# One core, linear attention into two mixtures of experts: where three engines scale the last rows, and eight dummy matmuls for fourteen

## The chip, the cores and the metric

The kernel runs on one core of a Trainium2 chip. A core has five engines, each with its own queue of instructions: TensorE (PE: matmuls and transposes; the profile lists its weight loads apart, as PEld), VectorE (DVE), ScalarE (ACT), GpSimd (POOL) and SyncE (SP, which here issues loads). They wait for one another by semaphores. The metric is the device time of one execution in microseconds (us); lower is better. TensorE's clock has two levels, and the profile gives the granted clock as a share of the full one: 1.00 is 2.4 GHz, 0.50 is 1.2 GHz.

## The reference

```
kv  = einsum('bhsd,bhse->bhde', k, v)         # 4 batches, 8 heads, 576 rows, 64 columns
out = q @ kv                                  # per batch and head
x   = out / sqrt(mean(out^2) + 1e-6) * g_norm # rows of 512 = 8 heads x 64
# mixture of experts, 8 experts, one per token (argmax of x @ w_gate), capacity limited
h = relu(x_e @ w1[e]);  y = h @ w2[e];  x = gate * y
# last layer: maximum of three products, then the output product
out = max(x @ m2w1, x @ m2w2, x @ m2w3) @ w_out    # 2304 x 512
```

## The kernel before, in words

The program has three parts. The first, up to about 91 us, is the attention: four batches one after another, each of 576 rows in five sets (set 0 has 64 rows, sets 1 to 4 have 128). The second, up to about 310 us, runs the experts, the fullest guess first; the third is the last layer. Only the first part and its seam to the second are touched.

For one batch `b` the engines do this. `kv_step` multiplies k and v on TensorE (`pk`, line 348). `out_step` transposes q in five pieces (`pq`, lines 375 and 380), which are copied out of PSUM as `qT`, some by ScalarE (line 386) and some by VectorE (line 384). `out_pair` and `out_rest` make the output products `po` (lines 436 and 408); ScalarE squares them (`sq`) and copies them (`ohl`). VectorE sums the squares (`ss`) and runs `stats_steps`: the norm factor `rnorm` (line 482), the logits (`lt`, `lg`), and the choice of expert (`eq` twice, `rm`, `oh`, lines 494 to 501). `normalise` then scales the five sets into `orow`: on GpSimd or VectorE one instruction for a set (line 516), on ScalarE eight (line 514, one for a head).

The routing of a batch stands inside the next batch's `out_pair`: TensorE makes `pp` (line 531) from `oh`, VectorE turns it into positions (`pt`, `jr`, `oht`, `ohsum`, `pos_i`), TensorE makes the census product `pc` (line 605) from `ohsum`, and VectorE goes on with `ch_v` and `pb`. `send` then hands five scatters of `orow` to memory (`xs`, line 538) to GpSimd's queue; each also waits for a ScalarE copy, so that they spread out.

The rows of the first expert don't go through memory for the later batches. For batches 0 and 1, `own_gather` gathers them back from `xs` into `oxg` (line 598, on GpSimd's queue); its indices are four small VectorE instructions, `og_u` to `og_i` (lines 592 to 595), and it waits for all scatters so far. For batches 2 and 3, `own` makes a 0/1 table on VectorE (`jl`, line 578, then `pick`, line 582), and TensorE picks the rows with it: 20 matmuls `px` (line 660), which the trace counts as 40 passes. For batches 0 and 1 TensorE transposes `oxg` (line 655). `own_out` copies each `px` as the high half (ScalarE, line 666) and the low half (VectorE, line 667) of `xt`, the input of the first expert.

Weights come from memory as raw tiles, four at a time in flight; `split_next` splits one half of a tile into a high part on ScalarE (line 297) and a low part on VectorE (line 298), and when both halves are done the next load is issued. Behind the last `xt`, VectorE makes `po_i` (line 1020), three register loads on ScalarE's queue read it, and then ScalarE copies the first product `ph` of the experts out as `h`.

Dummy matmuls of 128x128 (`keep_warm`, line 331, two passes each) stand at several places in the attention part.

The order on each engine is the order in which the code issues the instructions (the schedule is manual), so moving a call moves its instructions on every engine that it uses.

Of the kernel before, what the change touches and what calls it, by code (L numbers as in the profile page):

```python
# [9 lines left out]
F32 = mybir.dt.float32  # L10
# [11 lines left out]
B, H, S, D = 4, 8, 576, 64  # L22
# [18 lines left out]
def kernel(  # L41
# [16 lines left out]
    nc = tc.nc  # L58
# [40 lines left out]
    ps_o = stA.enter_context(tc.tile_pool(name="ps_o", bufs=6, space=PSUM))  # L99
# [228 lines left out]
    def keep_warm(p_, n):  # L328

        for _ in range(n):  # L330
            nc.tensor.matmul(p_[:, 0:128], ident, ident, start=True, stop=True)

    def kv_step(b):

        pk = ps_kv.tile([128, 4, D], F32, tag="pk", name=f"pk{b}")
        kt = [ins_t["k", b, u] for u in range(3)]
        vt = [ins_t["v", b, u] for u in range(3)]

        order = [(s, 4 * u + h) for u in range(2) for s in (1, 2, 3, 4) for h in range(4)]
        order += [(0, h) for h in range(H)]  # L340
        for s, h in order:
            if b == 0 and h % 4 == 0 and s == 1:
                keep_warm(ps_o.tile([128, 512], F32, tag="po", name=f"warm{h}"), 4 if h else 9)
            if b == B - 1 and h == 4 and s == 1:
                keep_warm(ps_o.tile([128, 512], F32, tag="po", name="warm3"), 8)
            l, r_ = (t_[h // 4][:, h % 4, s - 1, :] if s else t_[2][:, h, :] for t_ in (vt, kt))
            o_ = pk[h % 2 * D:h % 2 * D + D, h // 2, :]
            nc.tensor.matmul(o_, l, r_, start=s == 1 and h < 2, stop=s == 0 and h > 5)
        t_ = sa.tile([128, 4, D], F32, tag="kvT", bufs=1, name=f"kvT{b}")
        drip(b, nc.scalar.activation(out=t_, in_=pk, func=AF.Copy))  # L350
        kvT[b] = t_
# [14 lines left out]
    def out_step(b):  # L366
        qT = {}

        def tr(u):

            pq = ps_o.tile([128, 4, 128], F32, tag="po", name=f"pq{b}{u}")
            if u < 4:
                qm = ins_t["q", b, u % 2]
                for h in range(4):
                    nc.tensor.transpose(pq[:, h, :], qm[:, h, u // 2 * 2:u // 2 * 2 + 2, :], ident)
                n = 128
            else:
                n = D
                for j in range(4):
                    nc.tensor.transpose(pq[:, j, 0:D], ins_t["q", b, 2][:, 2 * j:2 * j + 2, :].rearrange(  # L380
                        "p h d -> p (h d)"), ident[:D, :D])
            t_ = sa.tile([128, 4, 128], F32, tag="qT", bufs=5, name=f"qT{b}{u}")[:, :, 0:n]
            if u == 2 or u == 4 and b < B - 1:
                nc.vector.tensor_copy(t_, pq[:, :, 0:n])
            else:
                i_ = nc.scalar.activation(out=t_, in_=pq[:, :, 0:n], func=AF.Copy)
                drip(b, i_)
            qT[u] = t_

        if b in (0, B - 1):  # L390
            keep_warm(ps_o.tile([128, 512], F32, tag="po", name=f"warmq{b}"), 10 if b == 0 else 6)
        tr(0)
        tr(2)
        if b == 0:
            keep_warm(ps_o.tile([128, 512], F32, tag="po", name="warmr"), 8)
        kvx_step(b)
        tr(1)
        tr(3)
        tr(4)
        return qT  # L400
# [103 lines left out]
    def rows_of(s):  # L504
        return 128 if s else D

    def normalise(b, s, eng):

        n = rows_of(s)
        i_ = ohl[b % 2][:n, s, :, 0:D]  # L510
        o_, r_ = orow[b % 2][:n, s].rearrange("p (h d) -> p h d", d=D), rnorm[b][:n, s]
        if eng is nc.scalar:
            for h in range(H):
                nc.scalar.activation(out=o_[:, h], in_=i_[:, h], func=AF.Copy, scale=r_[:, h:h + 1])
        else:
            eng.tensor_tensor(out=o_, in0=i_, in1=r_.unsqueeze(2).to_broadcast([n, H, D]), op=ALU.mult)
# [36 lines left out]
    def drip(b, i_):  # L553

        if pending:
            scatter(*pending.pop(0))
            after(xs_scatters[-1], [i_], "spread out")
# [29 lines left out]
    def own_gather():  # L587

        V = nc.vector
        u_, m_ = (sl_.tile([128, 2], F32, name=x) for x in ("og_u", "og_m"))  # L590
        i_ = sl_.tile([128, 2], I32, name="og_i")
        V.tensor_scalar(out=u_, in0=pb[:, 0:2], scalar1=slot[:, 0:1], scalar2=None, op0=ALU.add)
        V.tensor_tensor(out=m_, in0=u_, in1=pb[:, 1:3], op=ALU.is_lt)
        V.scalar_tensor_tensor(out=m_, in0=u_, scalar=eb0, in1=m_, op0=ALU.add, op1=ALU.mult)
        V.tensor_scalar_add(i_, m_, float(ZROW))
        for b in range(2):
            oxg[b] = sa.tile([128, DM], F32, tag="oxg", bufs=2, name=f"oxg{b}")
            g_ = nc.gpsimd.indirect_dma_start(
                out=oxg[b][:RB[b]].bitcast(I32), out_offset=None, in_=xs,
                in_offset=IndirectOffsetOnAxis(ap=i_[:RB[b], b:b + 1], axis=0))  # L600
            after(g_, xs_scatters, "rows come from every scatter")
# [62 lines left out]
    def own_out(b, px):  # L664
        at = slice(RO[b], RO[b] + RB[b])
        nc.scalar.activation(out=x0[:, :, 0, at], in_=px, func=AF.Copy, scale=g2)  # L666
        nc.vector.scalar_tensor_tensor(out=x0[:, :, 1, at], in0=px, scalar=g2, in1=x0[:, :, 0, at].bitcast(F32),
                                       op0=ALU.mult, op1=ALU.subtract)
# [12 lines left out]
    SORD = (0, 4, 1, 2, 3)  # L681
# [4 lines left out]
    def routes(b):  # L686
        route(b)
        send(b)

    def census_of(b):  # L690
        pcs[b] = census_pe(b)

    for b in range(B - 1):
        qT = out_step(b)
        out_pair(b, 0, qT, (lambda: routes(b - 1), lambda: census_of(b - 1)) if b else ())
        out_pair(b, 1, qT)
        out_rest(b, qT)
        load_batch(b + 2)
        if b:
            census(b - 1, pcs[b - 1])  # L700
        if b == 1:
            raw_upto(4)
        if b == 2:
            own_gather()
        for _ in stats_steps(b, 0, 5, rnorm[b]):
            pass
        for s in range(5):
            normalise(b, s, nc.gpsimd)
        kv_step(b + 1)
    b = B - 1  # L710
    qT = out_step(b)
# [15 lines left out]
    next(steps)  # L727
    for _ in steps:
        pass
    for s, eng in zip(SORD, (nc.scalar, nc.scalar, nc.gpsimd, nc.gpsimd)):  # L730
        normalise(b, s, eng)
    keep_warm(ps_o.tile([128, 512], F32, tag="po", name="warm6"), 4)
    pc = ps_kv.tile([128, NE], F32, tag="pm", name="pc")
    route(b)
# [3 lines left out]
    keep_warm(ps_o.tile([128, 512], F32, tag="po", name="warm7"), 3)  # L738
    own(b)
    send(b)  # L740
    normalise(b, SORD[4], nc.vector)
    for b_ in (2, 0, 1):
        own_out(b_, pxs[b_])
    split_next(4)
    own_out(b, own_pe(b))
    while pending:
        scatter(*pending.pop(0))
    stA.close()
# [327 lines left out]
    for j in range(NYB):  # L1076
# [20 lines left out]
        for g in range(NG):  # L1097
            jt = j * NG + g
            po = ps_tile(f"pz{jt}")
# [190 lines left out]
```

## Time and profile before

| | us |
|---|---|
| median of three runs | 658.71 (654.8 to 662.6) |
| the profiled execution | 655.94 |
| its span | 654.2 |

| engine | busy, us | share of the span |
|---|---|---|
| PE | 624.2 | 95% |
| DVE | 346.0 | 53% |
| ACT | 270.8 | 41% |
| POOL | 202.5 | 31% |

Times in all rows are counted from the start of the span. A row of the timeline has its start, how long it lasted from its first to its last instruction, the engine, the line, and behind `xN` in brackets how long the engine had been idle and what ended that. A row of the chain has the start and the length of one piece of the chain of work that ended last. A PE row's end is modelled.

### The profile page before, as it was taken

The numbers are of one execution on the slowest core, as the hardware profiler recorded it, in microseconds if no ns is written. First come the engines' busy times: TensorE is split into PE (matmuls) and PEld (weight loads), VectorE is DVE, ScalarE is ACT, GpSimd is POOL, SyncE is SP. The second block draws the span as 40 slices with busy tenths as digits, with TensorE's granted clock in tenths as the row PEclk, the third lists the DMA queues.
The fourth block names the chain that finished last, engine by engine and source line by source line (L and its number), as shares of the span: only waits on it lengthen the run. The fifth ranks groups of instructions, "written<-read, shape, count | busy, mean of one in ns | idle before, by whom it ended". The sixth has DMA issues, their size and how long they took to land.

```text
span 654.2 us, 11325 instructions
## 1 busy us (share of the span) xinstructions
PE 624.2 (95%) x4125; PEld 596.1 (91%) x4125; DVE 346.0 (53%) x719; ACT 270.8 (41%) x619; POOL 202.5 (31%) x280
## 2 busy tenths in 40 slices
PE   8889799989999999999999999999999999999992
PEld 8778798989999999998999989989989989999992
DVE  2576858786989898999965322222222221221220
ACT  1766544765756666676653221121121121121110
POOL 3274853213767685959500010010010001001001
PEclk9999789998999999999999999999999999999997
DMA  8999247866888887888862000000000000000000
GB/s 224 274 327 312 101 138 231 244 220 211 249 255 262 248 271 235 282 254 283 208 188 65 1 33 16 1 26 24 1 17 33 0 17 33 0 18 33 1 17 35
DMA packets 81661, 88.11 MB, mean 135 GB/s; under 512 B 15357, under 2 KB 71165, under 8 KB 81602
## 3 DMA queue, kind: packets, MB, share of 16 engines
q1 hardware_dynamic: 68448, 66.64, 34.8%
q0 software_dynamic: 6240, 14.41, 6.3%
q10 hardware_dynamic: 6914, 6.30, 2.8%
q8 instruction: 34, 0.56, 0.4%
q14 instruction: 25, 0.20, 0.1%
HBM read 71.56 MB, written 15.76 MB: 133 GB/s over the span
## 4 chain that ended last, share of the span: by engine, by line
PE 76%; DVE 9%; DMA 7%; issue 2%; ACT 2%; SPq 2%; ACTq 0%; POOL 0%; DVEq 0%; POOLq 0%
PE pa L762 11%; PE pa L764 11%; PE pa L763 11%; PE py L763 5%; PE py L764 5%; PE py L762 4%; PE pz L1104 4%; PE pz L1103 4%; PE pz L1105 4%; DMA raw<-in_moe_w_dram 3%; DVE w L298 3%; PE ph L764 3%; PE ph L763 3%; PE ph L762 3%; PE px L660 2%
## 5 line engine op out<-in xcount | busy, mean ns | idle before, releaser
L763 PE MATMUL pa<-ys,w 128*128 128x384 f32 x432 | 144.3, 334 | 0.0
L762 PE MATMUL pa<-ys,w 128*128 128x384 f32 x432 | 144.3, 334 | 0.0
L764 PE MATMUL pa<-ys,w 128*128 128x384 f32 x432 | 144.3, 334 | 0.0
L298 DVE TENSOR_TENSOR w<-raw,w 128x512 fp32r<-128x512 f32 x152 | 114.1, 779 | 26.8 <-ACT w L297 26.2
L1108 POOL DMA_INDIRECT out_dram<-o,ctab x18 | 17.5, 972 | 300.2 <-ACT o L1107 297.0
L1091 DVE TENSOR_TENSOR m<-pa,m 128x384 f32<-128x384 f32 x36 | 20.1, 558 | 138.3 <-PE pa L764 138.3
L297 ACT ACTIVATE w<-raw 128x512 fp32r<-128x512 f32 x152 | 89.4, 623 | 8.2 <-DMA raw<-in_moe_w_dram 8.2
L763 PE MATMUL py<-h,w 128*128 128x324 f32 (+7 forms) x256 | 80.9, 316 | 6.5 <-DVE h L786 6.5
L1093 ACT ACTIVATE g<-m 128x384 fp32r<-128x384 f32 x36 | 18.9, 526 | 151.3 <-DVE m L1092 151.3
L763 PEld LDWEIGHTS pa<-ys,w 128*128 128x128 f32 x432 | 81.1, 188 | 0.2
L762 PEld LDWEIGHTS pa<-ys,w 128*128 128x128 f32 x432 | 81.1, 188 | 0.2
L764 PEld LDWEIGHTS pa<-ys,w 128*128 128x128 f32 x432 | 81.1, 188 | 0.0
L763 PE MATMUL ph<-xt,w 128*128 128x324 f32 (+7 forms) x256 | 79.6, 311 | 0.8 <-DVE xt L678 0.6
L762 PE MATMUL py<-h,w 128*128 128x324 f32 (+7 forms) x256 | 80.3, 314 | 0.0
L762 PE MATMUL ph<-xt,w 128*128 128x324 f32 (+7 forms) x256 | 79.4, 310 | 0.6 <-ACT xt L666 0.6
L764 PE MATMUL py<-h,w 128*128 128x324 f32 (+7 forms) x256 | 79.9, 312 | 0.0
L764 PE MATMUL ph<-xt,w 128*128 128x324 f32 (+7 forms) x256 | 79.4, 310 | 0.0
L763 PEld LDWEIGHTS py<-h,w 128*128 128x128 f32 x256 | 48.8, 191 | 9.3 <-DVE h L786 9.1
L915 POOL TENSOR_TENSOR d<-d 128x256 f32<-128x256 f32 x48 | 31.7, 660 | 67.0 <-issue 18.6
L763 PEld LDWEIGHTS ph<-xt,w 128*128 128x128 f32 x256 | 48.3, 189 | 1.4 <-DVE xt L678 0.9
L762 PEld LDWEIGHTS ph<-xt,w 128*128 128x128 f32 x256 | 48.3, 189 | 0.9 <-ACT xt L666 0.8
L762 PEld LDWEIGHTS py<-h,w 128*128 128x128 f32 x256 | 48.7, 190 | 0.2
(247 smaller groups left out, 1052.7 us busy)
## 6 DMA issues: line engine op xcount, KB each, us to landing
raw<-in_moe_w_dram SPq DMA_DIRECT2D x64, 512.0 KB, 4.4
d<-in_moe_w_dram SPq DMA_DIRECT2D x36, 256.0 KB, 5.7
m2w<-dw ACTq DMA_DIRECT2D x36, 128.0 KB, 4.3
raw<-m2w SPq DMA_DIRECT2D x9, 512.0 KB, 4.6
k<-in_k_dram SPq DMA_DIRECT2D x8, 512.0 KB, 7.9
v<-in_v_dram SPq DMA_DIRECT2D x8, 512.0 KB, 9.6
q<-in_q_dram SPq DMA_DIRECT2D x8, 512.0 KB, 8.5
d<-in_moe_w_out_dram SPq DMA_DIRECT2D x12, 256.0 KB, 5.3
```

Source lines behind the costliest of these rows:

```text
L297: nc.scalar.activation(out=hi, in_=src, func=AF.Copy)
L298: (eng or nc.vector).tensor_tensor(out=lo, in0=src, in1=hi.bitcast(F32), op=ALU.subtract)
L762: nc.tensor.matmul(po, lhi, rhi, start=first, stop=False)
L763: nc.tensor.matmul(po, lhi, rlo, start=False, stop=False)
L764: nc.tensor.matmul(po, llo, rhi, start=False, stop=last)
L915: nc.gpsimd.tensor_tensor(out=lo.bitcast(F32), in0=hi.bitcast(F32), in1=lo.bitcast(F32), op=ALU.mult)
L1091: nc.vector.tensor_tensor(out=m_, in0=pa[1][:, :YB], in1=m_, op=ALU.max)
L1093: nc.scalar.activation(out=t_[:, 0], in_=m_, func=AF.Copy)
L1103: nc.tensor.matmul(po, h_[:, 0], w_[:, 0], start=c == 0, stop=False)
L1104: nc.tensor.matmul(po, h_[:, 0], w_[:, 1], start=False, stop=False)
L1105: nc.tensor.matmul(po, h_[:, 1], w_[:, 0], start=False, stop=c == NC2 - 1)
L1108: nc.gpsimd.indirect_dma_start(out=out, out_offset=IndirectOffsetOnAxis(ap=ctab[:, jt, 0:1].bitcast(I32), axis=0), in_=o_, in_offset=None)
```

## The change

Six edits, all in the attention part:

- In batch 2 the call of `own_gather` goes from ahead of `stats_steps` to behind `normalise`. So GpSimd scales the five sets of batch 2 ahead of the two gathers, and VectorE makes the four `og` indices behind `oh`.
- In batch 3 GpSimd scales no set: ScalarE takes three (0, 4, 1) where it took two, VectorE two (2, 3) where it took one.
- In batches 1 and 2 the third q piece (`u == 2`) is copied by ScalarE and not by VectorE.
- In batch 3 the eight dummies in the middle of `kv_step` become four, and stand ahead of its last eight products.
- The six dummies ahead of batch 3's transposes become four.
- Of the four splits ahead of the last `own_out`, two now stand behind it.

```diff
-            if b == B - 1 and h == 4 and s == 1:
-                keep_warm(ps_o.tile([128, 512], F32, tag="po", name="warm3"), 8)
+            if b == B - 1 and s == 0 and h == 0:
+                keep_warm(ps_o.tile([128, 512], F32, tag="po", name="warm3"), 4)
...
-            if u == 2 or u == 4 and b < B - 1:
+            if u == 2 and b in (0, B - 1) or u == 4 and b < B - 1:
...
-            keep_warm(ps_o.tile([128, 512], F32, tag="po", name=f"warmq{b}"), 10 if b == 0 else 6)
+            keep_warm(ps_o.tile([128, 512], F32, tag="po", name=f"warmq{b}"), 10 if b == 0 else 4)
...
-        if b == 2:
-            own_gather()
         for _ in stats_steps(b, 0, 5, rnorm[b]):
             pass
         for s in range(5):
             normalise(b, s, nc.gpsimd)
+        if b == 2:
+            own_gather()
...
-    for s, eng in zip(SORD, (nc.scalar, nc.scalar, nc.gpsimd, nc.gpsimd)):
-        normalise(b, s, eng)
+    for s in SORD[:3]:
+        normalise(b, s, nc.scalar)
...
-    normalise(b, SORD[4], nc.vector)
+    for s in SORD[3:]:
+        normalise(b, s, nc.vector)
     for b_ in (2, 0, 1):
         own_out(b_, pxs[b_])
-    split_next(4)
+    split_next(2)
     own_out(b, own_pe(b))
+    split_next(2)
```

On GpSimd, at the end of batch 2's statistics, before (the last scatter of batch 1 with the memset behind it, the two gathers, the five sets of batch 2, the first scatter of batch 2):

```order
L538 DMA xs<-orow_221,pos_i 18433x512
L544 MEMSET dummy 1x1
L598 DMA oxg_915<-xs,og_i 72x512
L598 DMA oxg_917<-xs,og_i 84x512
L516 TENSOR_TENSOR orow_220<-ohl_218,rnorm_224 64x512
L516 TENSOR_TENSOR orow_220<-ohl_218,rnorm_224 128x512 x4
L538 DMA xs<-orow_220,pos_i 18433x512
```

and after:

```order
L538 DMA xs<-orow_221,pos_i 18433x512
L544 MEMSET dummy 1x1
L516 TENSOR_TENSOR orow_220<-ohl_218,rnorm_224 64x512
L516 TENSOR_TENSOR orow_220<-ohl_218,rnorm_224 128x512 x4
L598 DMA oxg_940<-xs,og_i 72x512
L598 DMA oxg_942<-xs,og_i 84x512
L538 DMA xs<-orow_220,pos_i 18433x512
```

The five sets changed places with the two gathers; nothing else moved there.

On VectorE, behind the choice of expert of batch 2, before (the last two steps of the choice, the copy of a q piece of batch 3, and the start of batch 2's routing):

```order
L499 TENSOR_REDUCE rm_936<-eq_933 128x5
L501 TENSOR_TENSOR oh<-revb,rm_936 128x40
L384 COPY qT_1015<-pq_1010 128x512
L565 TENSOR_TENSOR pt_1069<-pp_1057,oh 128x40
L567 TENSOR_REDUCE jr_1071<-pt_1069 128x5
```

and after:

```order
L499 TENSOR_REDUCE rm_925<-eq_922 128x5
L501 TENSOR_TENSOR oh<-revb,rm_925 128x40
L592 TENSOR_SCALAR og_u<-pb,slot 128x2
L593 TENSOR_TENSOR og_m<-og_u,pb 128x2
L594 SCALAR_TENSOR_TENSOR og_m<-og_u,eb_201,og_m 128x2
L595 TENSOR_SCALAR og_i<-og_m 128x2
L384 COPY qT_1009<-pq_1004 128x512
L565 TENSOR_TENSOR pt_1063<-pp_1051,oh 128x40
L567 TENSOR_REDUCE jr_1065<-pt_1063 128x5
```

The four index instructions, which stood ahead of the whole statistics of batch 2, now stand between `oh` and the q copy.

On VectorE, at the seam to the experts, before (the low halves of `xt` for batches 1 and 3 with the four splits between them, then `po_i` and the low half of the first `h`):

```order
L667 SCALAR_TENSOR_TENSOR xt_234<-px_1164,g_92,xt_234 128x4x84
L298 TENSOR_TENSOR w_1259<-raw_685,w_1259 128x512
L298 TENSOR_TENSOR w_1262<-raw_685,w_1262 128x512
L298 TENSOR_TENSOR w_1267<-raw_697,w_1267 128x512
L298 TENSOR_TENSOR w_1270<-raw_697,w_1270 128x512
L667 SCALAR_TENSOR_TENSOR xt_234<-px_1275,g_92,xt_234 128x4x84
L1019 TENSOR_TENSOR po_f<-pb,roc 128x4
L1020 CAST po_i<-po_f 128x4
L786 SCALAR_TENSOR_TENSOR h_1368<-ph_1355,h_1368 128x324
```

and after (its lines from 742 on are numbered two higher):

```order
L667 SCALAR_TENSOR_TENSOR xt_234<-px_1158,g_92,xt_234 128x4x84
L298 TENSOR_TENSOR w_1260<-raw_685,w_1260 128x512
L298 TENSOR_TENSOR w_1263<-raw_685,w_1263 128x512
L667 SCALAR_TENSOR_TENSOR xt_234<-px_1268,g_92,xt_234 128x4x84
L298 TENSOR_TENSOR w_1291<-raw_697,w_1291 128x512
L298 TENSOR_TENSOR w_1294<-raw_697,w_1294 128x512
L1021 TENSOR_TENSOR po_f<-pb,roc 128x4
L1022 CAST po_i<-po_f 128x4
L788 SCALAR_TENSOR_TENSOR h_1369<-ph_1356,h_1369 128x324
```

The two splits of the second raw tile moved from ahead of the last `xt` to between it and `po_i`.

## Rows read from the trace of the kernel before

**Rows 1.** Windows: stretch, its length, each engine's busy us (instructions); PEclk, DMA, GB/s.

```profile
45.00:50.00 5.00, 3.12 (x33) 2.52 (x31) 4.68 (x13) 2.76 (x8) 4.19 (x5) 1.00 1.07 365
68.47:71.81 3.34, 0.00 (x1) 0.03 (x1) 3.31 (x3) 0.00 (x0) 3.17 (x4) 1.00 0.00 0
71.81:85.36 13.55, 13.55 (x80) 13.11 (x80) 9.32 (x24) 10.05 (x30) 7.03 (x12) 0.51 0.23 87
144.00:148.00 4.00, 2.04 (x8) 1.42 (x8) 3.93 (x9) 0.00 (x0) 1.68 (x2) 0.89 0.49 170
```

**Rows 2.** The chain that ended last, by time: start, length, engine and what.

```profile
64.90 0.18 PE pc L605
...
65.47 5.57 DVE jl L578
...
71.81 8.85 PE px L660 x40
80.66 1.04 PE px L655 x8
81.70 1.78 PE warm L331 x8
...
85.41 4.92 PE px L660 x40
...
90.93 0.57 DVE xt L667
...
106.72 9.06 DMA raw<-in_moe_w_dram
```

**Rows 3.** Timeline of POOL, around the gathers.

```profile
63.69 0.98 POOL L598 DMA_INDIRECT oxg<-xs,og_i  x1 [6.83 <-DMA xs<-orow,pos_i]
...
65.95 5.04 POOL L516 TENSOR_TENSOR orow<-ohl,rnorm 64x512 f32<-64x512 f32 x5
```

**Rows 4.** Timeline of VectorE: batch 1's `eq`, batch 2's and batch 3's statistics and routing.

```profile
45.34 0.90 DVE L494 TENSOR_TENSOR eq<-lg,mx 128x40 f32<-128x40 f32 x1
...
57.97 0.20 DVE L482 SCALAR_TENSOR_TENSOR rnorm<-u,r 128x40 f32<-128x40 f32 x1
...
59.74 0.20 DVE L494 TENSOR_TENSOR eq<-lg,mx 128x40 f32<-128x40 f32 x1
...
60.43 0.20 DVE L501 TENSOR_TENSOR oh<-revb,rm 128x40 bf16<-128x40 f32 x1
...
64.09 0.20 DVE L565 TENSOR_TENSOR pt<-pp,oh 128x40 f32<-128x40 f32 x1 [2.85 <-PE pp L531]
...
78.22 1.57 DVE L494 TENSOR_TENSOR eq<-lg,mx 128x40 f32<-128x40 f32 x1
...
80.29 0.20 DVE L501 TENSOR_TENSOR oh<-revb,rm 128x40 bf16<-128x40 f32 x1
...
84.29 0.29 DVE L578 TENSOR_SCALAR jl<-jr,base,pb 128x5 f32<-128x5 f32 x1
...
87.18 2.49 DVE L298 TENSOR_TENSOR w<-raw,w 128x512 fp32r<-128x512 f32 x4
...
91.60 0.18 DVE L1020 CAST po_i<-po_f 128x4 int32<-128x4 f32 x1
```

**Rows 5.** Timeline of PE: two waits of batches 1 and 2, batch 3's dummies.

```profile
31.23 1.09 PE L375 MATMUL pq<-ident,q 128*128 128x128 f32 x8 [0.98 <-DMA q<-in_q_dram]
...
49.90 0.17 PE L605 MATMUL pc<-ohsum,ones 128*128 128x8 bf16 x1 [0.39 <-DVE ohsum L549]
...
54.28 2.05 PE L331 MATMUL warm<-ident 128*128 128x128 f32 x16
...
57.95 1.60 PE L331 MATMUL warmq<-ident 128*128 128x128 f32 x12
```

**Rows 6.** Timeline of ScalarE: batch 3's sets, and the first `h`.

```profile
76.61 3.93 ACT L514 ACTIVATE orow<-ohl,rnorm 64x64 f32<-64x64 f32 x16 [0.92 <-ACT ohl L444]
...
94.28 0.44 ACT L785 ACTIVATE h<-ph 128x324 fp32r<-128x324 f32 x1 [3.38 <-issue]
```

## The prediction

> **What bounds the kernel now.** I read the page's slices first: TensorE (PE) is busy for 95% of the span, so a gain can come only from the few places where it waits or runs at the low clock. The windows find the dearest one at the end of the attention part. From 68.47 to 71.81 us PE does nothing (0.00 of 3.34 us busy), and from 71.81 to 85.36 it is busy throughout at a granted clock of 0.51, that is at the lower of its two levels, 1.2 of 2.4 GHz [rows 1]. The chain of waits says why: it runs through one VectorE (DVE) instruction, `jl` of line 578, for 5.57 us, then `pick`, then the 40 passes of the products `px` of batch 2 in 8.85 us; the same 40 passes of batch 3 take 4.92 us [rows 2].
>
> `jl` works on 128x5 numbers; its twin in batch 3 takes 0.29 us [rows 4]. What it waits for shows on GpSimd (POOL): there the five `orow` instructions of batch 2 run from 65.95 for 5.04 us, to 70.99, and `jl` ends at 71.04 [rows 2, 3]. POOL could have run them earlier, but before them stand the two gathers, which sat 6.83 us for the scatters of batch 1 to land [rows 3]. So one late block on POOL delays `jl`, and with it `pick`, PE, and the clock.
>
> The Trainium skill states in "GPSIMD Engine Reference", Key points, that GpSimd shares its SBUF interfaces with VectorE, with contention for VectorE instructions in a two-port mode or with two SBUF inputs. The trace agrees that such waits occur: `eq` takes 0.20 us beside an idle POOL, 0.90 and 1.57 beside `orow` [rows 4]. By that rule the moved block slows what it now lies beside, which speaks against the change; the next part prices it from rows alone.
>
> **The change, step by step.**
>
> *POOL's block ahead of the gathers.* `rnorm` of batch 2 ends at 58.17 now [rows 4]. The four small `og` instructions ahead of it, some 0.2 us each as `eq` is, go behind `oh`, so it ends at 57.4. The block of 5.04 us then runs from 57.5 to about 62.6. The gathers wait for the scatters until 63.69 anyway [rows 3], so POOL loses nothing: the block fills a wait. The cost falls on VectorE. `eq`, `eq` and `oh` of batch 2 now run beside `orow`. In batch 1, where they do so today, `eq` lost 0.7 us [rows 4]; three times that bounds the loss at 2.1. So `oh` comes at about 61.9, where it is at 60.6 now [rows 4]. Behind it stands `og_u`, a TENSOR_SCALAR as `jl` is: either it is held to the end of the block, 62.6, or it starts at once. I take the first, since `jl` is the nearest row. With 0.8 us of `og` and 0.7 of the `qT` copy behind it, VectorE's routing instructions start at 64.1 (63.4 if it isn't held), where they start at 64.09 now [rows 4]. So `jl` starts where it does now, at 65.5, but takes 0.3 us instead of 5.57. `pick` is done by 66.5, before PE asks for it.
>
> *The dummies.* Eight ahead of the second half of line 348's products took 2.05 us, six behind them 1.60 [rows 5]; four and four cost 1.0 and 1.1, so PE saves 1.5 us. It can't keep that. Its census product `pc` comes at 64.90 now [rows 2] and needs `ohsum`, 0.8 us behind the start of VectorE's routing, so it comes at 64.9 again, and PE waits about 1.5 us ahead of it. I count the dummies as 0 us; the bounds are -0.7 (`og_u` not held) and +0.5 (the block longer beside VectorE's work).
>
> *The q copy on ScalarE (batches 1 and 2).* It costs ScalarE about 0.5 us ahead of `kvx` in each, and takes as much off VectorE ahead of `pt`. In batch 2 PE waited 0.39 us for `ohsum`, just ahead of 49.90 [rows 5]. That is the most it can bring: -0.4 us. Since PE waits again at `pc` of batch 3, I take 0. In batch 1 PE waits 0.98 us for q's loads at that place [rows 5], which covers ScalarE's 0.5; without that cover it would cost 0.5.
>
> *What follows from `jl`.* PE goes from its last `po`, at 68.47, straight to `px`: the idle 3.34 us go [rows 1]. With no such gap I expect the full clock to hold: from 45 to 50 us PE was busy for only 3.12 of 5 us and kept it [rows 1]. Then `px` takes 4.92 instead of 8.85 (-3.93), the 8 passes of L655 half of 1.04 (-0.5), the dummies behind them half of 1.78 (-0.9), and the routing between them and the last `px` some 0.15 less [rows 2]. Sum: 3.34 + 3.93 + 0.5 + 0.9 + 0.15 = 8.8 us.
>
> *Does VectorE keep up?* PE would ask for batch 3's `oh` when its dummies end, now 83.48 (81.70 + 1.78) and then 74.7. `oh` ends at 80.49 now [rows 4], so it has to come 5.8 us sooner. Its chain queues behind `jl` and `pick` and moves up by the 5.3 us that `jl` loses, and `eq` in it loses 1.37 of its 1.57 us, as POOL does no `orow` of batch 3 any more [rows 4]: 6.7. It keeps up, by 0.9 us.
>
> *Batch 3's sets.* ScalarE took 3.93 us for two sets, from 76.61 [rows 6], so 5.9 for three; 5.3 sooner, they run from 71.3 to 77.2. PE's last `px` starts 8.8 sooner than 85.41, at 76.6, and needs the third set 16 of 40 passes later, at 78.6. VectorE's two sets follow `pick`; at POOL's 1.01 us each (5.04 / 5 [rows 3]), which bounds them from above, they end by 78.6, and PE needs the first of them at 79.6. Both are hidden, by 1 us or more.
>
> *The weights.* Two of the four splits now stand behind the last `xt`. ScalarE is idle there. On VectorE, two of the four L298 (2.49 us [rows 4]) now lie ahead of `po_i`, and three register loads and the first `h` on ScalarE wait for that: `po_i` at 91.60, `h` at 94.28 [rows 4, 6]. So `h` stands 1.25 us further behind the last `xt` than now. From `h` on, the chain goes through the splits and the weight loads and not through PE, until 147 us; one load in it alone is 9.06 us [rows 2]. So I count +1.25 in full; 0 is the other bound.
>
> **Sum.** -8.8 + 1.25 = -7.55 us. The profiled execution took 655.94 us (span 654.2), so 648.4. It lies 2.8 us below the median of the three runs (658.71; 654.8 to 662.6), on which the sum would be 651.2. I say 649.8, between the two.
>
> **The rivals.**
>
> *A: the clock falls at the new wait (ends slower).* Fewer dummies, and 1.5 us of waiting ahead of `pc`. From 144 to 148 us PE was busy for 2.04 of 4 us, and the granted clock fell, to 0.89 in the mean [rows 1]. If that happens at `pc`, and `px` doesn't bring the clock back (it did not from 71.81 to 80.66 [rows 1, 2]): `po`, 3.6 us from 64.90, becomes 6.4 (by 8.85 / 4.92), to 71.3; `px` 8.85, to 80.2; 1.04 and 1.78, to 83.0; routing 1.93 (83.48 to 85.41), to 84.9; `px` 4.92 or 8.85, to 89.8 or 93.8, against 90.33 now. With the +1.25 that is +0.7 to +4.7: 656.6 to 660.6, middle 659. It decides if the wait at `pc` comes near 2 us. Against it: 1.88 us of idling in the 5 us from 45 left it at 1.00 [rows 1]. Chance 0.16. [...]
>
> *B: PE starts 8.8 us sooner, the weights don't follow.* The second raw tile is freed 1.25 us behind the last `xt` instead of 1.3 us ahead of it (87.18 + 2.49 against 90.93 [rows 2, 4]), so the load that takes its place comes 2.5 us later against the products. If that reaches the splits in full, on top of the +1.25, the gain is 5: 651 on the profiled run's scale, 654 on the median's. For it: the chain behind the first `h` hangs on such loads. Against it: two other raw tiles are split first. Chance 0.12.
>
> *C: the change doesn't free `jl`*, because something else held it, such as the gathers, which now come just ahead of it. Then `px` starts at 71.8 as before and only +1.25 is left: 657. The ends of `orow` at 70.99 and of `jl` at 71.04 speak against it: 0.04.
>
> *D: more than counted.* `og_u` isn't held (-0.7), the q copy's 0.4 us arrive, the +1.25 hides: 9 to 10 us, 646. Chance 0.08.
>
> **How the numbers follow.** The likeliest course has 0.60, with gains of 6.6 to 8.6 us: 647.3 to 652.1 over both scales. The range reaches down to D (645.5) and up into A's lower part (657.5). It leaves out A's upper half. A measurement of this kernel can tell about 1%, 6.6 us, from no change. Faster by over 1%: most of the likeliest (0.53 of 0.60) and D (0.08), 0.61. Slower by over 1%: only A at its worst with a further loss of 2 us, 0.05. Within 1%: 0.34.
>
> **What would show it.** `orow` of batch 2 on POOL from 57.5 to 62.6 and the gathers near 63.7; `jl` under 1 us; no idle PE ahead of `px`; both `px` groups near 4.9 us; a granted clock of 1.00 from 60 to 92 us; the first `ph` near 82.1 and the first `h` near 86.7. A low clock between 65 and 85 us, or a first `ph` later than 85, makes me wrong; a first `ph` at 82 with a gain under 5 us means B.

## The result, and the profile after

The changed kernel took 646.7 us in the median (644.1 to 654.1, 20 runs), the kernel before, timed beside it, 656.4 us (20 runs). The ratio is 0.985, with a 95% interval of 0.983 to 0.988: a gain of 9.7 us, where 649.8 us had been forecast from a base of 655.9 to 658.7, with a gain of 7.55 us. Medians here are of all executions; ratios leave out those more than 1.5% above the fastest of their kernel. The profiled execution has a span of 645.0 us, where it was 654.2.

The same windows as in [rows 1] show the gain. Columns as there; the second stretch is now the wait ahead of `pc` of batch 3, the third runs from the first `px` of batch 2 to the last `px` of batch 3. This is the changed kernel.

```profile
45.00:50.00 5.00, 3.59 (x32) 3.02 (x33) 4.59 (x11) 4.82 (x11) 3.77 (x4) 1.00 1.09 346
65.42:66.86 1.44, 0.00 (x1) 0.00 (x0) 1.37 (x7) 0.91 (x2) 0.99 (x1) 1.00 0.51 161
70.36:83.35 12.99, 12.33 (x120) 11.83 (x119) 9.68 (x27) 9.99 (x35) 8.76 (x16) 1.00 0.34 122
144.00:148.00 4.00, 4.00 (x31) 3.97 (x30) 3.16 (x7) 3.61 (x9) 1.82 (x2) 1.00 0.83 259
```

Both groups of `px`, all that lies between them and the routing now fit into 12.99 us at a clock of 1.00. Before, the 13.55 us at 0.51 held only the first `px` and the steps up to the second. (The row at 144 us lies among the experts, where executions of one kernel differ too.)

The chain of work of the changed kernel, in order of time (start, length, engine and what):

```profile
63.94 0.98 DVE og_u L592
...
70.43 4.78 PE px L660 x40
75.21 0.55 PE px L655 x8
75.76 0.93 PE warm L331 x8
...
78.53 4.83 PE px L660 x40
...
85.88 1.16 DVE po_i L1022
...
114.68 6.05 DMA raw<-in_moe_w_dram
```

Against [rows 2]: `jl` of batch 2 is gone from the chain, the first `px` takes 4.78 us for 8.85, and two new VectorE entries have come, `og_u` and `po_i`, each about 1 us. POOL's timeline tells what each of these two waited for:

```profile
59.60 5.28 POOL L516 TENSOR_TENSOR orow<-ohl,rnorm 64x512 f32<-64x512 f32 x5 [0.71 <-DVE rnorm L482]
65.86 1.00 POOL L598 DMA_INDIRECT oxg<-xs,og_i  x1 [0.99 <-DVE og_i L595]
67.17 0.96 POOL L598 DMA_INDIRECT oxg<-xs,og_i  x1 [0.30 <-issue]
...
86.03 0.97 POOL L887 MEMSET y<- 128x1008 f32 x1
```

and VectorE's shows the instructions beside it:

```profile
61.02 0.91 DVE L494 TENSOR_TENSOR eq<-lg,mx 128x40 f32<-128x40 f32 x1
61.97 0.97 DVE L496 TENSOR_TENSOR eq<-eq,revw 128x40 f32<-128x40 f32 x1
...
63.20 0.74 DVE L501 TENSOR_TENSOR oh<-revb,rm 128x40 bf16<-128x40 f32 x1
63.86 1.04 DVE L592 TENSOR_SCALAR og_u<-pb,slot 128x2 f32<-128x2 f32 x1
...
67.34 0.28 DVE L578 TENSOR_SCALAR jl<-jr,base,pb 128x5 f32<-128x5 f32 x1
...
85.88 1.15 DVE L1022 CAST po_i<-po_f 128x4 int32<-128x4 f32 x1
```

POOL's block ends at 64.88, `og_u` at 64.90. `jl` takes 0.28 us although a gather stands beside it on POOL's queue, from 67.17 to 68.13. `po_i` ends at 87.03, POOL's MEMSET at 87.00.

On PE, the two waits that are left around the change:

```profile
66.86 0.17 PE L605 MATMUL pc<-ohsum,ones 128*128 128x8 bf16 x1 [1.44 <-DVE ohsum L549]
...
78.53 4.82 PE L660 MATMUL px<-pick,orow 64*128 64x84 f32 x40 [0.66 <-DVE pos_i L572]
```

and on ScalarE, the three sets and the first `h`:

```profile
73.21 5.84 ACT L514 ACTIVATE orow<-ohl,rnorm 64x64 f32<-64x64 f32 x24 [0.92 <-ACT ohl L444]
...
89.06 0.44 ACT L787 ACTIVATE h<-ph 128x324 fp32r<-128x324 f32 x1 [4.10 <-PE ph L766]
```

Times by the clock of the span mislead here, because the loads bring batch 2 in at another time in each execution: its `pc` came at 48.9 to 54.0 us in the profiles of this study that the second table lists. So I measure from that `pc` to the first `ph`. That stretch took 41.06 us before and takes 32.06 after.

| stretch, us | before | after | difference |
|---|---|---|---|
| start to `pc` of batch 2 | 49.90 | 51.92 | +2.02 |
| to the first `ph` | 41.06 | 32.06 | -9.00 |
| to the first `h` | 3.32 | 5.08 | +1.76 |
| to the end | 559.96 | 555.90 | -4.06 |

The first and the last row differ as much between two executions of one kernel: three profiles of the changed kernel have 50.5 to 54.0 and 555.9 to 559.2 there, the two of the kernel before 49.9 and 52.9, and 560.0 and 557.4. Only the two rows in the middle can be put down to the change as they stand; 0.37 us of it also lies ahead of `pc` of batch 2 (the q copy, below).

### The profile page after: what moved, and what is told of

It reads as the page before. It is cut to its first block, busy times and chain, and to the rows that moved or that the text cites. A ratio compares the mean times of both kernels' runs of the same rounds, so it can differ in the third digit from the quotient of the medians.

```text
span 645.0 us, 11307 instructions
## 1 busy us (share of the span) xinstructions
PE 616.2 (96%) x4113; PEld 588.9 (91%) x4113; DVE 343.4 (53%) x718; ACT 273.7 (42%) x629; POOL 199.9 (31%) x278
## 4 chain that ended last, share of the span: by engine, by line
PE 78%; DVE 11%; DMA 4%; issue 2%; ACT 2%; ACTq 0%; SPq 0%; POOL 0%; POOLq 0%; DVEq 0%
PE pa L764 12%; PE pa L766 12%; PE pa L765 12%; PE py L765 5%; PE py L766 5%; PE py L764 5%; PE pz L1106 4%; PE pz L1105 4%; PE pz L1107 4%; PE ph L766 3%; PE ph L765 3%; PE ph L764 3%; DVE w L298 3%; PE pxt L774 2%; PE po L436 2%
## 5 line engine op out<-in xcount | busy, mean ns | idle before, releaser
L765 PEld LDWEIGHTS py<-h,w 128*128 128x128 f32 x256 | 48.3, 189 | 8.3 <-DVE h L788 8.1
L765 PEld LDWEIGHTS ph<-xt,w 128*128 128x128 f32 x256 | 48.3, 189 | 0.8 <-DVE xt L667 0.4
L766 PEld LDWEIGHTS ph<-xt,w 128*128 128x128 f32 x256 | 48.3, 189 | 0.7 <-DVE w L298 0.7
L764 PEld LDWEIGHTS ph<-xt,w 128*128 128x128 f32 x256 | 48.2, 188 | 0.8 <-ACT xt L666 0.8
```

What stands on the lines that cost most here:

```text
L764: nc.tensor.matmul(po, lhi, rhi, start=first, stop=False)
L765: nc.tensor.matmul(po, lhi, rlo, start=False, stop=False)
L766: nc.tensor.matmul(po, llo, rhi, start=False, stop=last)
```

## The experiments

After the result I had one theory and several rivals. **T1**: the place of POOL's block is the gain, the rest only rides along. The rivals: that the gain came with the other edits, that the dummies or splits matter, and later, that it is chance of one chip.

### Four kernels on one chip, and a stall that I had not looked for

The block alone, put into the kernel before:

```diff
-        if b == 2:
-            own_gather()
         for _ in stats_steps(b, 0, 5, rnorm[b]):
...
             normalise(b, s, nc.gpsimd)
+        if b == 2:
+            own_gather()
```

> The kernel before with one edit alone: in batch 2 POOL's five orow instructions stand ahead of the two gathers. Theory 1 (the block held jl, and all of the gain comes from that): nearly the whole gain of 9.7 us (656.4 to 646.7), so 645 to 649; jl under 1 us, no idle PE ahead of px, both px groups near 4.8 us. Two sets of batch 3 stay on POOL, so eq of batch 3 may take 1.6 us again, which moves pp by no more than 0.5 us. Theory 2 (the gain is spread over the six edits): 651 to 654.

The reverse, that edit undone in the changed kernel (the same diff with its signs turned):

> The changed kernel with that one edit undone: the gathers stand ahead of POOL's block of batch 2 again, the other five edits stay. Theory 1: jl takes over 5 us again, PE idles over 3 us ahead of px, the granted clock falls to 0.5 for some 10 us, and the time is that of the kernel before, 655 to 658. Theory 2: 649 to 652.

The fourteen dummies of before in the changed kernel:

```diff
-            if b == B - 1 and s == 0 and h == 0:
-                keep_warm(ps_o.tile([128, 512], F32, tag="po", name="warm3"), 4)
+            if b == B - 1 and h == 4 and s == 1:
+                keep_warm(ps_o.tile([128, 512], F32, tag="po", name="warm3"), 8)
...
-            keep_warm(..., 10 if b == 0 else 4)
+            keep_warm(..., 10 if b == 0 else 6)
```

> The changed kernel with batch 3's dummies as before: eight in the middle of kv_step and six ahead of the transposes, instead of four and four. Theory 1 (PE only waits less at pc, where it waited 1.44 us in the changed kernel's trace): the wait ahead of pc shrinks to about 0, and the time stays within 0.5 us of 646.7. Theory 3 (the dummies' 1.5 us of PE time are part of the gain): 648.2.

And none of the eight that the changed kernel has there:

```diff
-            if b == B - 1 and s == 0 and h == 0:
-                keep_warm(ps_o.tile([128, 512], F32, tag="po", name="warm3"), 4)
...
-        if b in (0, B - 1):
-            keep_warm(..., 10 if b == 0 else 4)
+        if b == 0:
+            keep_warm(..., 10)
```

> The changed kernel with none of those eight dummies. PE reaches pc some 2 us earlier and waits about 3.5 us instead of 1.44. Theory 1 with the clock holding: 646.7 again. My rival A (a longer wait at pc drops the clock): the granted clock falls to 0.5 at about 65 us, px of batch 2 takes 7 to 9 us, and the time is 650 to 657.

Measured, with the kernel before at 656.5 us beside them: 659.4 (ratio 1.004, 1.002 to 1.007), 656.9 (1.001, 0.999 to 1.004), 656.2 (1.000, 0.997 to 1.002) and 656.5 us (1.002, 0.999 to 1.006). None gained anything, not even the two that differ from the changed kernel by six or eight dummies. What was expected of the first and the third was far off; the other two came out where one theory had them, but, as it turned out, for another reason.

Their profiles share something that neither first profile has. In batch 3's `kv_step` TensorE's products come one or two at a time, about 0.72 us apart or twice that, from about 56 to 60 us (58.9 to 62.5 with the block put back). One row tells it; this is the kernel with the block alone, PE from 52 to 62 us by line (busy and mean ns of one, then the idle time ahead and what ended it):

```profile
L348 PE MATMUL pk<-k,v 128*64 128x64 f32 x32 | 2.3, 228 | 2.8 <-issue 2.8
```

"issue" is idle time for which the trace names no cause. From `pc` of batch 2 to that of batch 3 these four kernels took 18.7 to 21.3 us, where both first profiles took 15. With batch 3 that late, POOL's block is over before VectorE comes to `jl`, wherever the block stands, so these runs can't tell its place. The two counts of dummies, 14 and none, came out the same beside each other, but only with the stall.

Theory P was that the stall belongs to these programs, theory Q that it belongs to the chip that they ran on.

### The changed kernel and the kernel before, once more

Both unchanged, on another chip.

> The changed kernel once more, unchanged, beside the kernel before on the same chip. Theory P (the stall of some 4 us that the four kernels so far showed in batch 3's products, TensorE's pk at L348 at one per 0.7 us from 55.9 to 60.1 us, belongs to their layouts of the program and not to the chip): no such stall, pc of batch 3 at 66.9 us, span 645, time 645 to 649, ratio to before 0.983 to 0.988. Theory Q (it belongs to the chip that those four ran on, and whoever runs there has it): if it runs on such a chip, the stall is there, pc at 72 to 75 us, time 655 to 658.

> The kernel before, with a profile from this chip. Theory P: pc of batch 3 at 64.9 us as in its first profile, jl held for over 5 us, px at 71.8 us at half clock, span about 654. Theory Q: the pk products stall from about 55 to 60 us, pc of batch 3 at 70 us or later, and jl then short, since the POOL block is done by then.

The changed kernel took 648.0 us against 656.2 (ratio 0.9885, 0.984 to 0.993), with no stall, and the stretch from `pc` of batch 2 to the first `ph` took 32.06 us, to the hundredth as in its first profile. The kernel before, with 657.5 us in its one run, had neither the stall nor a long `jl`. Its POOL, from the gathers on:

```profile
66.84 0.98 POOL L598 DMA_INDIRECT oxg<-xs,og_i  x1 [7.02 <-DMA xs<-orow,pos_i]
...
69.11 5.03 POOL L516 TENSOR_TENSOR orow<-ohl,rnorm 64x512 f32<-64x512 f32 x5
```

its VectorE at that place:

```profile
69.33 4.84 DVE L549 TENSOR_TENSOR ohsum<-ohsum,oht 128x8 bf16<-128x8 bf16 x1
```

and the windows of its wait and of what followed:

```profile
69.30:74.20 4.90, 0.23 (x2) 0.04 (x2) 4.87 (x3) 1.05 (x3) 4.85 (x5) 0.97 0.13 37
74.20:80.80 6.60, 6.57 (x38) 5.87 (x37) 4.13 (x10) 2.74 (x7) 4.63 (x8) 0.50 0.28 99
```

The gathers waited 7.02 us for the scatters, the block came behind them, and this time `ohsum`, four instructions ahead of `jl`, was the one beside it. PE stood still ahead of `pc` and then made `po` at half clock instead of `px`. The stretch took 41.52 us, about as long as with a held `jl` (41.06); but 1.67 us of it lie earlier, between `pc` of batch 2 and batch 3's first `pk` (4.97 us for 3.30), where the clock had been at 0.50 from 53.5 to 56.5 us. So the kernel before pays for the block whichever instruction meets it, though not the same amount.

### The same two kernels with and without the block's move, on a third chip

The changed kernel, the block alone in the kernel before, and the changed kernel with the block put back, side by side. The diffs are those of the first two experiments.

> The changed kernel a third time, beside the two that follow, on one chip. Theory Q (the stall of TensorE's pk products, one per 0.72 us from 56 to 60 us, that the first four experiments showed, belongs to the chip that they ran on): with a profile that has no such stall, pc of batch 3 at 65 to 67 us, span 645, time 645 to 649; on a chip that has it, pc at 72 to 74 us and time 655 to 658. Theory P (the stall belongs to the layout of those programs): no stall here on any chip, 645 to 649 us.

> The kernel before with one edit: the POOL block of batch 2 ahead of own_gather. The same kernel as the first experiment, beside the changed kernel on one chip. Theory Q: without the stall, ohsum ahead of pc or jl is no longer held for 5 us, px of batch 2 at 69 to 72 us with 4.85 us, span 645 to 649, time 647 to 651, ratio to before 0.985 to 0.992. Theory P: the stall is there as in the first experiment, pc at 72 to 73 us, time 655 to 660, whatever the changed kernel does beside it.

> The changed kernel with that one edit undone: own_gather ahead of the POOL block of batch 2. The same kernel as the second experiment. Theory T1 (the place of the block is what the change gains): the block starts when the scatters of batch 1 have landed and holds jl or ohsum for about 5 us, px of batch 2 follows an idle PE of over 3 us and one of px or po runs at half clock, time 654 to 658. Theory T2 (the gain is elsewhere, in the sets, splits or dummies): time 646 to 650.

Measured: 646.8 us (ratio 0.984, 0.979 to 0.990), 651.3 us (0.990, 0.986 to 0.995) and 655.0 us (0.997, 0.994 to 1.000), with the kernel before at 656.5. No profile has the stall; the row from above reads, for the block alone, PE from 50 to 60 us:

```profile
L348 PE MATMUL pk<-k,v 128*64 128x64 f32 x64 | 2.3, 225 | 0.0
```

The same two programs stalled on the first chip and not on this one, which is for Q: the stall went with the chip, or the hour, and not with the program. Its cause stays open. Neither the changed kernel nor the kernel before has a profile from the first chip, so how they would stand there is not known, beyond the 656.5 us that the kernel before took.

With the block put back, T1 came out (654 to 658), in a third way. POOL, then VectorE, then PE of that kernel:

```profile
68.48 5.04 POOL L516 TENSOR_TENSOR orow<-ohl,rnorm 64x512 f32<-64x512 f32 x5
```

```profile
70.32 3.25 DVE L472 TENSOR_SCALAR ms<-ss 128x40 f32<-128x40 f32 x1
```

```profile
69.60 1.12 PE L660 MATMUL px<-pick,orow 64*128 64x84 f32 x8 [0.42 <-POOL orow L516]
73.58 7.12 PE L660 MATMUL px<-pick,orow 128*128 128x84 f32 x32 [2.86 <-POOL orow L516]
```

The routing was through before the block began; now `px` itself waits for the sets that POOL hasn't scaled yet, 0.42 and 2.86 us, and goes on at half clock:

```profile
73.58:80.70 7.12, 7.12 (x34) 7.12 (x35) 3.22 (x11) 6.17 (x26) 5.35 (x10) 0.50 0.40 147
```

The block alone brought only a part: 5.2 us where the changed kernel beside it brought 9.7, by the medians, or 6.3 of 10.4 by the ratios. The intervals of the two ratios overlap, so the size of that part is uncertain, but the profile shows a place where time is lost. POOL, VectorE and PE in batch 3:

```profile
75.61 2.04 POOL L516 TENSOR_TENSOR orow<-ohl,rnorm 128x512 f32<-128x512 f32 x2
```

```profile
75.27 2.41 DVE L578 TENSOR_SCALAR jl<-jr,base,pb 128x5 f32<-128x5 f32 x1
```

```profile
78.47 9.02 PE L660 MATMUL px<-pick,orow 64*128 64x84 f32 x40 [2.78 <-DVE pos_i L572]
```

The first `px` ran at 4.85 us, as forecast. But batch 3 then comes sooner, and its own `jl` meets the two sets that POOL still scales in the kernel before: 2.41 us instead of 0.29, PE waits 2.78 us, and the clock falls, for this `px` and beyond:

```profile
78.47:87.49 9.02, 9.01 (x40) 8.64 (x40) 4.30 (x8) 0.00 (x0) 7.46 (x10) 0.50 0.56 168
```

### The sets of batch 3 back on GpSimd

So the second edit, no set of batch 3 on POOL, was tried by itself:

```diff
-    for s in SORD[:3]:
-        normalise(b, s, nc.scalar)
+    for s, eng in zip(SORD, (nc.scalar, nc.scalar, nc.gpsimd, nc.gpsimd)):
+        normalise(b, s, eng)
...
-    for s in SORD[3:]:
-        normalise(b, s, nc.vector)
+    normalise(b, SORD[4], nc.vector)
```

> The changed kernel with one edit undone: GpSimd scales two sets of batch 3 again, ScalarE two, VectorE one. Theory S (with the block ahead of the gathers, the next hold is the one by these two sets: in the kernel with the block alone, jl of batch 3 took 2.42 us beside them, TensorE waited 2.8 us for pos_i ahead of the last px, and the clock went to half for 13.7 us, so that this px took 9.02 us): jl of batch 3 at 2 us or more, the last px starts 2 us or more behind the routing that it waits for, first ph 2 to 5 us later than in the changed kernel at the same pc of batch 3, time 649 to 652 us. Theory N (the sets are hidden wherever they run): jl of batch 3 at 0.3 us, last px 4.8 us, time 646 to 648 us.

It took 648.8 us against 655.5 (ratio 0.989, 0.983 to 0.994). POOL, VectorE and PE:

```profile
75.77 2.05 POOL L516 TENSOR_TENSOR orow<-ohl,rnorm 128x512 f32<-128x512 f32 x2
```

```profile
75.94 1.91 DVE L578 TENSOR_SCALAR jl<-jr,base,pb 128x5 f32<-128x5 f32 x1
```

```profile
78.63 7.84 PE L660 MATMUL px<-pick,orow 64*128 64x84 f32 x40 [2.28 <-DVE pos_i L572]
```

This is theory S, nearly to its numbers: `jl` 1.91 us, PE waits 2.28 us, the last `px` takes 7.84 us; the time lies just below the 649 to 652 us that S gave. From `pc` of batch 3 the first `ph` comes after 21.76 us, where the changed kernel needs 17.12: 4.6 us later. (Another 1.5 us of its 38.18 in the table below lie ahead of that `pc`, in a fall of the clock that the edit doesn't reach.) Its windows, the wait for `oh` ahead of `pc` of batch 2, a stretch behind that `pc`, and the last `px`:

```profile
46.00:47.70 1.70, 0.00 (x1) 0.00 (x0) 1.63 (x4) 0.91 (x2) 1.70 (x3) 1.00 1.08 359
50.00:52.00 2.00, 2.00 (x10) 2.00 (x10) 1.22 (x1) 1.19 (x4) 1.78 (x4) 0.50 1.24 180
78.63:86.47 7.84, 7.84 (x40) 7.54 (x40) 3.11 (x6) 0.00 (x0) 6.27 (x11) 0.59 0.49 165
```

Against the 646.8 us of the changed kernel on that chip 2 us of it show at the end; the interval holds the whole loss and none alike, so the place is shown by the profile, and the size of what reaches the end is not.

### The gathers later, and the splits back

The gathers and their indices behind batch 2's routing:

```diff
-        if b == 2:
-            own_gather()
...
-    out_pair(b, 0, qT, (..., lambda: (census(b - 1, pcs[b - 1]), own(b - 1))))
+    out_pair(b, 0, qT, (..., lambda: (census(b - 1, pcs[b - 1]), own(b - 1), own_gather())))
```

> The changed kernel with own_gather issued later still, in batch 3's first pair of products, behind the routing of batch 2. Theory T1 (the hold of og_u, 1.04 us, is all that the gathers' place still costs): og_u no longer holds ohsum, so TensorE's wait of 1.44 us ahead of pc goes, and the time is that of the changed kernel less 0.5 to 1.4 us. Theory T2 (the gathers' data is then late for the first h): first h 2 to 5 us later, time 648 to 652.

It took 650.6 us (ratio 0.991, 0.987 to 0.995, the kernel before at 656.2). PE's wait for `ohsum` went, but PE then waited at other places:

```profile
61.77 1.09 PE L375 MATMUL pq<-ident,q 128*128 128x128 f32 x8 [0.35 <-DMA q<-in_q_dram]
63.24 0.46 PE L380 MATMUL pq<-ident,qx 64*128 64x64 f32 x4 [0.37 <-DMA qx<-in_q_dram]
...
74.79 0.44 PE L655 MATMUL px<-ident,oxg 72*128 72x72 f32 x4 [0.69 <-DMA oxg<-xs,og_i]
75.91 0.48 PE L655 MATMUL px<-ident,oxg 84*128 84x84 f32 x4 [0.68 <-ACT orow L514]
```

With 0.36 us for a load of v, PE waited 1.08 us for loads, and `pc` of batch 3 came 14.96 us behind that of batch 2, where it came after 14.94 with the wait. And the gathers' rows were late for the transposes of line 655. T2 held: the first `h` came 2.5 us later behind `pc` of batch 2.

The four splits ahead of the last `own_out` again:

```diff
-    split_next(2)
+    split_next(4)
     own_out(b, own_pe(b))
-    split_next(2)
```

> The changed kernel with the four splits of batch 3 ahead of own_out again (po_i behind them). Theory T1 (two splits ahead of own_out and two behind it only trade the start of px3 against the first h): px3 waits 1.3 us longer for pos_i and the first h comes about as in the changed kernel, time within 1 us of it. Theory T2 (the splits behind own_out cost 1.25 us at the first h): time 1.2 us less than the changed kernel's.

It took 649.4 us (ratio 0.987, 0.983 to 0.992), beside 648.0 for the changed kernel. The first `h` came 3.85 us behind the first `ph`, where it took 5.08 to 5.13 in the three profiles of the changed kernel: 1.23 us or a little more, as T2 said, and the last `px` started with the same 0.66 us of waiting as without the edit (here for ScalarE's `orow`, there for `pos_i`), so the splits' place bought nothing there. One reason is that `po_i` now falls ahead of POOL's MEMSET:

```profile
86.22 0.17 DVE L1021 CAST po_i<-po_f 128x4 int32<-128x4 f32 x1
```

Yet the time didn't fall by 1.2 us; the intervals are too wide to say more. This profile was disturbed earlier, where the edit doesn't reach. The windows are PE's wait for a load of q in batch 3, the stretch behind it, and the next:

```profile
60.39:62.06 1.67, 0.01 (x1) 0.00 (x0) 1.60 (x4) 1.09 (x4) 1.67 (x3) 0.98 1.05 366
62.06:68.80 6.74, 6.74 (x38) 6.11 (x39) 3.13 (x13) 2.94 (x7) 2.77 (x3) 0.50 0.75 237
68.80:72.00 3.20, 3.20 (x36) 2.83 (x35) 3.03 (x6) 3.12 (x9) 2.05 (x4) 1.00 0.18 41
```

A wait of 1.67 us, and the clock went to half for 6.7 us.

All profiles without the stall, side by side (us):

| kernel | `pc` 2 to `pc` 3 | `px` of batch 2 | PE waits ahead of the last `px` | last `px` | `pc` 2 to first `ph` |
|---|---|---|---|---|---|
| before, two profiles | 15.00, 21.35 | 8.85, 4.85 | none, 0.7 | 4.96, 4.82 | 41.06, 41.52 |
| changed, three profiles | 14.94 to 14.96 | 4.85 | 0.66 | 4.82 | 32.06, 32.06, 32.07 |
| block alone | 15.00 | 4.85 | 2.78 | 9.02 | 38.44 |
| changed, block back | 13.52 | 11.10 | 0.66 | 7.61 | 41.53 |
| changed, sets back | 16.43 | 4.85 | 2.28 | 7.84 | 38.18 |
| changed, gathers later | 14.96 | 4.85 | none | 4.89 | 34.54 |
| changed, splits back | 18.18 | 4.85 | 0.66 | 4.82 | 35.64 |

## Why the prediction held, step by step

**POOL's block.** It was to start 7.6 us behind `pc` of batch 2 (57.5 less 49.90) and started 7.68 behind it, took 5.28 us for 5.04, and the gathers came 13.94 us behind that `pc`, where they came after 13.79 [rows 3]; they now wait for `og_i` and no longer for the scatters. The loss on `eq`, `eq` and `oh` was bounded at 2.1 us; they took 0.91, 0.97 and 0.74 for 0.20 each, 2.0 more. `og_u` was taken as held to the end of the block, and was: it took 1.04 us, where it takes 0.22 in the kernel before. `jl` fell to 0.28 us beside a gather, which refutes rival C.

**The dummies and `pc`.** PE was to lose its 1.5 us again ahead of `pc`; it waited 1.44 there. Three profiles agree: with the block's move and fourteen dummies `pc` of batch 3 came 15.00 us behind that of batch 2, with the move and eight after 14.94, and with eight and no move, so that no `og_u` holds the routing, after 13.52. No run without the stall has another count of dummies and nothing else changed. The lower bound, -0.7 us without the hold of `og_u`, was too hopeful in the one kernel that tried it: the loads of q were the next limit.

**From `jl` to the first `ph`.** 8.8 us were counted, 9.00 measured. By its terms, against [rows 1, 2]: the idle 3.34 us went; `px` 8.85 to 4.78 (-4.07 for -3.93); L655 1.04 to 0.55 (-0.49); the dummies 1.78 to 0.93 (-0.85); the routing the rest. VectorE kept up: PE does not wait for batch 3's `oh`. ScalarE's three sets took 5.84 us for 5.9, hidden.

**Rival A**, the clock falling at the new wait, did not come in three profiles of the changed kernel, with waits of 1.1 to 1.5 us at `pc`; the clock was 1.00 from 60 to 92 us in each. It was nearer than that makes it sound: the clock did fall after 1.67 us without work in the kernel with the splits back, and with the sets back after 2.28 us and once after 1.70.

**The step that was right in its sum and incomplete in its reason** is the second edit. The prediction counted the sets of batch 3 only as work that ScalarE and VectorE can hide, and gave their leaving POOL a worth in one place, `eq`, 1.37 us [rows 4]. It did not ask what POOL's two sets would do beside the routing of batch 3 once that comes sooner. They hold `jl` of batch 3 for 1.9 to 2.4 us, PE waits 2.3 to 2.8 us, and the clock goes. The block alone brings the stretch from 41.1 or 41.5 to 38.4 us, about 3; all the other edits without it leave it at 41.5; together they bring it to 32.1, about 9. Each of the two middle figures is one profile, and in time the second edit shows as less: 2.0 us between the sets back and the changed kernel, and 4.5 between the block alone and all six. The sum of 8.8 us was correct because both edits were in the change, but "one late block on POOL delays `jl`, and with it the clock" is only the first of two such blocks.

**The splits.** +1.25 us at the first `h`; undoing the edit gave back 1.23. In the first pair of profiles it was +1.76, in the pair from one chip +1.08 (4.03 to 5.11). That the size fits is largely luck. About 1 us of it is `po_i` meeting a MEMSET, which the prediction did not see: with the sets back and with the block put back the splits stand in the same place, POOL's MEMSET is over before `po_i`, and the first `h` comes 4.06 us behind the first `ph`. With all four splits ahead it came after 3.32 to 4.03 us in four profiles. So the splits themselves cost between nothing and 0.7 us. Rival B, weights that don't follow, fell: the stretch from the first `h` to the end is not longer (555.9 to 559.2 us for 557.4 and 560.0).

**The q copy** was counted at nothing, because PE waits again at `pc` of batch 3. It was not tried alone, but the traces show its place: from the first `pp` that waits for `oh` to `pc` of batch 2, first in the kernel before, then in the changed one:

```profile
48.30 0.17 PE L531 MATMUL pp<-oh,tri_s 128*128 128x8 bf16 x1 [1.04 <-DVE oh L501]
```

```profile
50.69 0.17 PE L531 MATMUL pp<-oh,tri_s 128*128 128x8 bf16 x1 [1.70 <-DVE oh L501]
...
51.92 0.17 PE L605 MATMUL pc<-ohsum,ones 128*128 128x8 bf16 x1
```

That is 1.60 us before [rows 5] and 1.23 after, without the wait of 0.39; all three profiles with that copy on VectorE have 1.60, all seven with it on ScalarE 1.22 or 1.23. The stretch behind that `pc` gave none of it back (14.94 us to `pc` of batch 3, for 15.00). So the term was worth about 0.4 us, as far as the loads, which move batch 2 by 5 us between executions, let it through.

**The time.** Forecast 649.8, measured 646.7, 648.0 and 646.8 us. The base is 0.9 us of the difference: I placed the sum between the profiled run and a median of three runs, 658.71, and the kernel before took 655.5 to 656.5 us in every later set; on 656.4 the sum gives 648.9. The rest is a gain of 8.2 to 9.7 us for 7.55. The rows give 9.00, and 0.37 for the q copy, less 1.08 to 1.76 at the first `h`: 7.6 to 8.3 us. What is left, up to 2 us, lies in stretches that differ by more than that between executions of one kernel, and no run here places it. Rival D's 646 is the nearest number, but of its three conditions only the q copy's came.

The signs that were given in time from the start of the span served badly: the first `ph`, forecast near 82.1 us, with anything later than 85 as a miss, came at 83.98, 82.56 and 86.06 in the three profiles of the changed kernel, while its distance from `pc` of batch 2 was the same.

## What to carry to other kernels

When an engine is freed of a late block, list what it does next beside the work that now comes sooner: taking one hold away let the next one bite, and in one profile each the first edit alone brought a third of what all brought in that stretch, the rest without it nothing. A block whose start hangs on a transfer (here scatters landing) meets another instruction in each execution, `ohsum`, `jl` or the product itself, so look for what starts it, not for the instruction that waits. And where loads shift the start of a stage by several us between executions, compare lengths from a mark inside the program, and repeat a surprising experiment on another chip beside its control before building on it.

## What the runs showed of the hardware

**Where a held VectorE instruction ends.** In each of these seven cases of a long hold it ends 0.02 to 0.05 us behind the end of the work on POOL, whatever its own size:

| held, kernel | ends | POOL's work ends |
|---|---|---|
| `jl`, before | 71.04 | 70.99 |
| `ohsum`, before, second profile | 74.17 | 74.14 |
| `ms`, block back | 73.57 | 73.52 |
| `jl` of batch 3, block alone | 77.68 | 77.65 |
| `jl` of batch 3, sets back | 77.85 | 77.82 |
| `og_u`, changed | 64.90 | 64.88 |
| `po_i`, changed, beside a MEMSET | 87.03 | 87.00 |

`ohsum` and `ms` were held through the rest of a block of five POOL instructions, `jl` through a whole one. One of these doesn't fit wholly: `jl` in the kernel before starts at 65.47, 0.48 us ahead of POOL's first set, and why it had not ended by then, in the 0.28 us that it takes elsewhere, no run shows. `eq` and `oh` (TENSOR_TENSOR, 128x40) instead got in before the block was over, after 0.7 to 1.0 us each, and `lg`, a TENSOR_REDUCE, was hardly slowed: 0.75 us beside the block of the changed kernel, 0.74 in the kernel before, where POOL stood idle. But `eq` of batch 3 in the kernel before, 1.57 us [rows 4], ended 0.06 us behind the second of POOL's two sets, having started beside the first. The Trainium skill, "SBUF — State Buffer", Who interferes with whom, says that VectorE and GpSimd share a port pair as an exclusive lock, that TENSOR_SCALAR, copy and cast can take part in it as well as instructions with two SBUF inputs, and TENSOR_REDUCE not. The trace agrees on the kinds: the held ones in the table are TENSOR_SCALAR, TENSOR_TENSOR and CAST, and TENSOR_REDUCE took 0.75 us for 0.74. The same section of the Trainium skill has whoever issues first hold the ports for its whole instruction; here a hold went on through several GpSimd instructions in a row, for 4.84 and 5.57 us, and the measurement decides. Why `eq` mostly gets in where `ohsum` and `jl` don't, no run here shows. A DMA that POOL only issues held nothing: `jl` took 0.28 us beside a gather of 0.96 us.

**TensorE's clock.** Ahead of its falls in batch 3 PE had been idle for 1.67, 2.28, 2.78, 2.86, 3.34 and 4.7 us, in six profiles without the stall. After 1.13, 1.26, 1.44 and 1.46 us at `pc` it stayed at full. One wait comes out both ways: ahead of the first `pp` in batch 2 PE stood idle for 1.70 us in six profiles; the clock stayed at 1.00 behind it in four of them (the changed kernel twice, the block put back, the gathers later) and fell to 0.50 in two (from 53.5 to 56.5 us in the second profile of the kernel before, from 49.5 to 52.5 us with the sets back). So the length of one wait doesn't decide alone. Once at half it stayed there through 9.01 us of busy `px` with the block alone, and through 6.57 and 6.74 us of other products.

**A stall without a name.** On one chip four programs had TensorE's products at one or two per 0.72 us for some 4 us in one place, while ScalarE too did nothing for 4.1 to 4.3 us; the same two programs that were repeated on another chip had none. Such a profile says nothing of the edit, and the cause of the stall is open.
